# Attention with mixed heads and a two-layer MLP on one core: the step planner counts TensorE's instructions in blocks of 256 and gets new ranks

## The chip, the cores and the metric

The kernel runs on one core of a Trainium2 chip. The metric is device time in microseconds (us), measured outside the profiler; lower is better. Profiles are single executions, so their times are compared with their own span.

## What is computed

```python
def _attn_ref(q, k, v, w_pre, w_post):            # q, k, v: (4, 12, 448, 64) float32
    scale = 1.0 / np.sqrt(q.shape[-1])
    scores = scale * np.matmul(q, k.transpose(0, 1, 3, 2))
    scores = np.einsum('bhij,hg->bgij', scores, w_pre)     # heads mixed, 12 x 12
    scores = scores - np.max(scores, axis=-1, keepdims=True)
    attn = np.exp(scores)
    attn = attn / (np.sum(attn, axis=-1, keepdims=True) + 1e-09)
    attn = np.einsum('bhij,hg->bgij', attn, w_post)        # heads mixed again
    return np.matmul(attn, v)

def _moe_ref(x, U, V, w_ch1, w_ch2):              # x: (4, 448, 768), weights float64
    h = x.transpose(0, 2, 1) @ U @ V              # U 448 x 32, V 32 x 448
    u = x + h.transpose(0, 2, 1)
    return u + np.maximum(u @ w_ch1, 0.0) @ w_ch2 # 768 -> 3072 -> 768
```

The attention output of a batch, heads side by side, is the x of the second function.

## The kernel before

**Two stages.** The first is the attention with its two head mixings; the second is the MLP, with each weight split into a high and a low part and three matmuls for every product (`up`, `dn`). The first stage works in chunks of 10 query rows: 180 chunks over 4 batches, gathered into 17 units of 6 to 12 chunks; two chunks make one `premix`/`postmix` pair, k = 0 to 89. The second runs over 24 slices f of the hidden dimension and the 4 batches b.

**The steps of the first stage, in the order of the data** (line numbers as in the profile):
- `q`, `k`, `v` loads on SP's DMA queue (L378, L371, L498). The k tile of a batch comes in parts, for batches 1 to 3 in six of one head pair each.
- `qk` (TensorE, L394): scores of a unit's rows for one head pair (two pairs in the first two units), into a PSUM bank. `qk_out` (ACT or DVE, helper lines L302/L304) copies the bank into an `s` tile; there are 3 of these.
- `relay` (SP queue, for the first two units half of them on ACT's, L405): two DMAs for each head pair, which carry the s tile to a `t` tile in the layout that the mixing wants. There are two t tiles, which alternate by unit: the relays of unit u can start only when the last `premix` of unit u-2 is done.
- `premix` (TensorE, L432) mixes the heads into a bank; `max` (DVE, L437), two `exp` (ACT, L442), `eps` (POOL, L446), `recip` (DVE, L449), `scale` (POOL, L453) follow; `postmix` (TensorE, L467, 56 small matmuls, each with a weight load) mixes again into another bank; `post_out` (ACT or DVE, L302/L304) copies that into an `a` tile.
- `av` (TensorE, L509 and L517) multiplies with v, twice per unit; `av_out`, `av_add` bring it into the accumulator. When a batch is complete, `tp`, `t1`, `hp` (L707, L724, L738) apply U and V.

All of TensorE's steps share 4 PSUM bank pairs (`bank_58` to `bank_61` in the rows of the order).

**What sets the order.** Nothing is reordered when the kernel runs: each engine and each DMA queue takes its instructions in the order in which they were written. The class `Plan` writes it while the kernel is built. It plays the steps through with a price for each (a table in the code, in ns) and, whenever an engine is free, takes the ready step of lowest rank whose buffers and bank are free. The ranks come from the table `RANK`, in units of chunks. For the change these matter: `qk_lead` and `qk_step` (how many chunks before the unit's first chunk its qk steps are ranked), `kr` and `qr` (how much earlier the loads of k and q are ranked, and at which `premix` they are let go), `av_off` and `av_step` (how long after a unit's last chunk its av steps come), `post`, `ex`, `qo`, and for the first two units `k0`, `kstep`, `k1`. The second stage from f = 2 on follows lists of its own for PE, ACT, DVE and POOL (`plan.lines`), which the change does not touch.

The price of a step on TensorE before was a number alone, with one addition for an engine that had stood idle:

```python
                    if e == "PE" and now - free[e] > 600:
                        cost += min(cost, 850)
```

Of the kernel before, what the change touches and what calls it, by code (L numbers as in the profile page):

```python
# [18 lines left out]
B, H, S, D = 4, 12, 448, 64  # L19
# [11 lines left out]
AV = 3  # L31
# [14 lines left out]
class Unit:  # L46
# [12 lines left out]
RANK = dict(  # L59
    m0=16.083, mb=7.238, mf=2.802, e0=-45.773, estep=6.06, er=6.491, ne=8, qk_lead=5.047, qk_step=0.857, av_off=4.137,  # L60
    av_step=0.796, post=4.408, kr=4.245, vr=7.776, qr=5.202, mx=0.98, ex=1.029, ep=3.308, po=2.298, qo=0.448, 
    uv0=4.57, uvs=0.155, uv1=2.315, u0=-2.242, us=7.039, w0=2.447, w1=22.727, up=-0.694, raw=8, even=2, ga=-0.14, k0=-14.744, kstep=-0.114, k1=8.823,
)
# [28 lines left out]
class Plan:  # L92
# [5 lines left out]
    LATENCY, PE_LATENCY = 128, 196  # L98
    DMA_START, DMA_DONE = 650, 910

    def __init__(self, rings, banked, banks, weight):
# [16 lines left out]
    def take(self, s):  # L118
        ring = self.bank_free if s[0] in self.banked else self.rings[s[0]]
        self.where[s] = ring.pop(0)  # L120

    def order(self):
        steps, users = self.steps, dict(self.users)
# [16 lines left out]
        for k, n in wait.items():  # L140
            if n == 0:
                push(k, 0)

        place = {k: (n, i) for n, line in enumerate(self.lines) for i, k in enumerate(line)}
# [26 lines left out]
        while events:  # L171
# [28 lines left out]
            while moved:  # L200
                moved = False
                for e in free:
# [20 lines left out]
                    if e == "PE" and now - free[e] > 600:  # L223
                        cost += min(cost, 850)
                    if e in self.port[k]:
                        cost += max(0, shared - now)
                        shared = now + cost
# [18 lines left out]
def build(tc, q2, kt, vj, wpre_in, wpost_in, u_in, v_in, ident, w1j, w2, out, show=None):  # L246
# [230 lines left out]
    for k in range(NC // 2):  # L477
        r = 2 * k
        us = sorted({chunks[2 * k][0], chunks[2 * k + 1][0]})
        pre, post, st, e, wr = ("pre", k), ("post", k), ("st", k), ("e", k), ("wr", k)  # L480
        ts = [("t", u) for u in us]
        plan.add(("premix", k), [("PE", 770)], partial(premix, k=k), r, ["wpre", ("zero", 0), ("zero", 1)] + [("relay", u, h) for u in us for h in range(H)], [pre] + ts)
        plan.add(("max", k), [("DVE", 1000)], partial(neg_max, k=k), r + RANK["mx"], [("premix", k)], [pre, st], port=())
        for i in range(2):
            plan.add(("exp", k, i), [("ACT", 622)], partial(exp, k=k, i=i), r + RANK["ex"], [("max", k)], [pre, st, e])
        plan.add(("eps", k), [("POOL", 120)], partial(add_eps, k=k), r + RANK["ep"], [("exp", k, i) for i in range(2)], [st], port=())
        plan.add(("recip", k), [("DVE", 80)], partial(recip, k=k), r + RANK["ep"], [("eps", k)], [st], port=())
        plan.add(("scale", k), [("POOL", 330)], partial(scale_w, k=k), r + RANK["ep"], ["wpost", ("recip", k)], [st, wr], port=BOTH)
        plan.add(("postmix", k), [("PE", 815)], partial(postmix, k=k), r + RANK["post"], [("scale", k)], [e, wr, post])
        for js in ([(0, 1)] if len(us) == 1 else [(0,), (1,)]):  # L490
# [42 lines left out]
    for u, un in enumerate(units):  # L533
# [4 lines left out]
        for p in range(0, H // 2, AV):  # L538
            r = rank_av(u, p)
            z = ("av", (u, p))  # L540
            plan.add(("av", u, p), [("PE", 300 + AV * 610)], partial(av, u=u, p=p), r, [("v", un.b, p + c) for c in range(AV)] + [("post_out", c) for c in range(first[u], first[u + 1]) if ("post_out", c) in plan.steps],
                     [(f"vr{p // AV}", un.b), (f"a{tn(u)}", u), z])
            plan.add(("av_out", u, p), OUT(AV * un.rows), partial(av_out, u=u, p=p), r + 0.65 * AV, [("av", u, p)], [z], port=())
            plan.add(("av_add", u, p), [("DVE", 75 + 1.042 * AV * un.rows // 2)], partial(av_add, u=u, p=p), r + 0.65 * AV, [("av_out", u, p)], [z], port=())
# [400 lines left out]
```

## Time and profile before

| | us |
|---|---|
| time, median of 3 runs | 1080.75 |
| lowest and highest of them | 1076.23, 1084.03 |
| the profiled execution: its own time | 1082.24 |
| its span, first to last instruction | 1080.4 |
| TensorE busy in the span | 1038.6 (96%) |
| DVE, ACT, POOL busy | 679.1, 402.4, 274.2 |
| TensorE's matmuls, weight loads, semaphore rows (counts) | 12240, 12240, 272 |

The page of the profile gives busy time by engine and in 40 slices; other views give waits (who stood idle, and what ended the idle time), a timeline of instructions, the chain of work that ended last, and the busy time in chosen stretches with the clock that TensorE was granted (PEclk, as a share of 2.4 GHz) and the share of the 16 DMA engines. The ends of matmuls are modelled: a matmul is shown as busy until about 0.2 us after the next one could start, so a wait shown as 0.7 us is a gap of about 0.9 us from start to start. "issue" as the releaser of a wait means that no semaphore event ended it.

### The profile page before, as it was taken

Reading aid. Unit: us, or ns where it says so; the run is one execution under the profiler, and the core shown is the slowest. Engines: PE = TensorE matmul, PEld = TensorE weight load, DVE = VectorE, ACT = ScalarE, POOL = GpSimd, SP = SyncE. Lnnn points to the kernel's source line nnn. Section 1 sums busy time; section 2 is a strip of 40 time slices with the busy share of each in tenths; the row PEclk is TensorE's granted clock in tenths of the full one; section 3 lists DMA queues with packets and bytes.
Section 4 is the critical chain, followed back from the end, with each engine's and each line's share of the span. In section 5 each row is a group of like instructions: output and inputs, shape, how many; then the busy total and the mean of one; then the engine's idle time right before and its main releaser. Section 6 shows DMA issues by size and latency. Waiting matters only on the chain.

```text
span 1080.4 us, 28693 instructions
## 1 busy us (share of the span) xinstructions
PE 1038.6 (96%) x12240; PEld 880.4 (81%) x12240; DVE 679.1 (63%) x1091; ACT 402.4 (37%) x844; POOL 274.2 (25%) x395
## 2 busy tenths in 40 slices
PE   4798999999989999999999999999999999999998
PEld 1465666765656788999999999999999999999998
DVE  2274575576567979666666666666666666666635
ACT  1785777667757832122122112221222122212200
POOL 3131111111213813232223223332232233322300
PEclk8999999999999999999999999999999999999999
DMA  6674546545666212121121112211221122212105
GB/s 182 203 202 136 175 143 187 179 140 173 178 192 180 69 52 89 47 71 55 49 59 59 48 56 59 59 59 44 59 59 48 55 59 59 59 44 60 45 1 204
DMA packets 59511, 105.25 MB, mean 97 GB/s; under 512 B 11816, under 2 KB 43768, under 8 KB 59384
## 3 DMA queue, kind: packets, MB, share of 16 engines
q1 hardware_dynamic: 58544, 102.14, 31.9%
q8 instruction: 96, 1.57, 0.6%
q10 hardware_dynamic: 840, 1.29, 0.4%
q14 instruction: 31, 0.25, 0.1%
HBM read 57.62 MB, written 7.08 MB: 60 GB/s over the span
## 4 chain that ended last, share of the span: by engine, by line
PE 88%; DMA 5%; ACT 2%; DVE 2%; issue 1%; SPq 1%; POOL 0%; ACTq 0%; DVEq 0%
PE bank L780 32%; PE bank L800 32%; PE bank L467 6%; PE bank L509 6%; PE bank L394 5%; PE bank L432 4%; DMA t<-s 3%; PE bank L517 1%; ACT e L442 1%; DMA k<-in_kt 1%; PE bank L724 1%; SPq L405 1%; PE bank L707 1%; DMA kr<-in_v 1%; ACT a L302 1%
## 5 line engine op out<-in xcount | busy, mean ns | idle before, releaser
L803 DVE TENSOR_TENSOR acc<-acc,bank 128x896 f32<-128x896 f32 (+1 forms) x153 | 163.7, 1071 | 161.3 <-PE bank L800 160.7
L785 ACT ACTIVATE hh<-bank 128x448 fp32r<-128x448 f32 x96 | 52.3, 545 | 469.0 <-PE bank L780 300.6
L800 PE MATMUL bank<-hh,w1h 128*128 128x448 f32 x576 | 209.1, 363 | 0.0
L780 PE MATMUL bank<-uh,w0h 128*128 128x448 f32 x576 | 209.1, 363 | 0.0
L780 PE MATMUL bank<-ul,w0h 128*128 128x448 f32 x576 | 208.8, 362 | 0.0
L800 PE MATMUL bank<-hl,w1h 128*128 128x448 f32 x576 | 208.7, 362 | 0.0
L780 PE MATMUL bank<-uh,w0l 128*128 128x448 f32 x576 | 207.8, 361 | 0.8 <-POOL w0l L309 0.8
L800 PE MATMUL bank<-hh,w1l 128*128 128x448 f32 x576 | 207.5, 360 | 0.0
L640 POOL TENSOR_TENSOR a<-a,x 128x384 f32<-128x384 f32 (+2 forms) x98 | 98.5, 1005 | 404.7 <-DVE x L636 402.5
L467 PEld LDWEIGHTS bank<-wr,e 60*64 60x64 f32 x5040 | 91.8, 135 | 49.8 <-issue 32.0
L437 DVE TENSOR_REDUCE mx<-bank 128x2 f32<-128x896 f32 x90 | 97.3, 1087 | 36.1 <-PE bank L432 31.1
L442 ACT ACTIVATE e<-bank,mx 128x448 f32<-128x448 f32 x180 | 113.3, 641 | 12.7 <-DVE mx L437 9.3
L800 PEld LDWEIGHTS bank<-hl,w1h 128*128 128x128 f32 x576 | 108.1, 188 | 8.4
L780 PEld LDWEIGHTS bank<-ul,w0h 128*128 128x128 f32 x576 | 108.2, 188 | 8.3
L780 PEld LDWEIGHTS bank<-uh,w0l 128*128 128x128 f32 x576 | 107.7, 187 | 8.6 <-POOL w0l L309 1.0
L800 PEld LDWEIGHTS bank<-hh,w1l 128*128 128x128 f32 x576 | 107.7, 187 | 7.8 <-issue 0.4
L800 PEld LDWEIGHTS bank<-hh,w1h 128*128 128x128 f32 x576 | 108.2, 188 | 5.7
L780 PEld LDWEIGHTS bank<-uh,w0h 128*128 128x128 f32 x576 | 108.1, 188 | 5.7
L467 PE MATMUL bank<-wr,e 60*64 60x60 f32 x5040 | 95.7, 220 | 10.5 <-issue 8.0
L394 PE MATMUL bank<-k,q 64*64 64x448 f32 (+3 forms) x768 | 94.6, 560 | 11.6 <-DMA k<-in_kt 8.2
L789 DVE SCALAR_TENSOR_TENSOR hl<-bank,hh 128x448 fp32r<-128x448 f32 x96 | 60.0, 625 | 66.6 <-ACT hh L785 66.6
L432 PE MATMUL bank<-t,wpre 64*64 64x448 f32 x720 | 87.6, 550 | 13.7 <-DMA t<-s 7.0
(62 smaller groups left out, 1121.6 us busy)
## 6 DMA issues: line engine op xcount, KB each, us to landing
t<-s SPq DMA_DIRECT2D x108, 210.0 KB
kr<-in_w1j SPq DMA_DIRECT2D x48, 384.0 KB
kr<-in_w SPq DMA_DIRECT2D x48, 384.0 KB
v<-in_vj SPq DMA_DIRECT2D x24, 256.0 KB
t<-s SPq DMA_DIRECT2D x24, 192.5 KB
k<-in_kt SPq DMA_DIRECT2D x19, 224.0 KB
t<-s SPq DMA_DIRECT2D x24, 175.0 KB
out<-acc SPq DMA_DIRECT2D x9, 448.0 KB
```

The costliest lines, as they stand in the source:

```text
L394: eng.matmul(o[64 * j:64 * j + at.stop - at.start, i, :S], lhsT=q[d, pp, at], rhs=k[d, pp, :], start=True, stop=True)
L432: eng.matmul(o[64 * j:64 * j + 64, i, :S], lhsT=wpre[64 * i:min(64 * i + 64, QW)], rhs=tt[tn(u)][64 * i:min(64 * i + 64, QW), n, :], start ...
L437: eng.tensor_reduce(out=mx, in_=T["pre", k][:, :, :S], axis=AX.X, op=ALU.max, negate=True)
L442: eng.activation(out=e[:, i], in_=T["pre", k][:, i, :S], func=ACTF.Exp, bias=T["mx", k][:, i:i + 1], accum_out=sm[:, i:i + 1])
L467: eng.matmul(d, lhsT=e[64 * j:64 * j + HALF, i, x * KB:x * KB + KB], rhs=wr[64 * j:64 * j + HALF, i].rearrange("p (g m) -> p g m", m=MH), ...
L509: eng.matmul(main[i * D:(i + 1) * D, c, :n], lhsT=v[:, c, i, x, :], rhs=a[:, x * H + 2 * (p + c) + i, :n], start=(c == 0 and x == 0), stop ...
L640: eng.tensor_tensor(out=f32(a), in0=f32(a), in1=f32(x), op=ALU.add)
L780: eng.matmul(ps, lhsT=w[:, c * 128:(c + 1) * 128], rhs=u[:, c, :], start=(i == 0), stop=(i == 3 * KC - 1))
L785: eng.activation(out=hh, in_=T["up", f, b], func=ACTF.Relu)
L789: eng.scalar_tensor_tensor(out=hl, in0=T.pop(("up", f, b)), scalar=0.0, in1=f32(T["hh", f, b]), op0=ALU.max, op1=ALU.subtract)
L800: eng.matmul(ps[:, j, :S], lhsT=w[:, (c + j) * 128:(c + j + 1) * 128], rhs=h, start=(i == 0), stop=(i == len(todo) - 1))
L803: eng.tensor_tensor(out=two(b, c, n), in0=two(b, c, n), in1=T.pop(("dn", f, b, c))[:, :n, :S], op=ALU.add)
```

## The change

Three things are changed in the planner, and none in what a step does. The planner now counts TensorE's instructions and, 258 instructions after the place 190 of each block of 256 (at the count 448 from that block's start), holds TensorE until 4000 ns have passed since that place (`fetched`). Some prices are new (`premix`, `eps`, `postmix`, and `av`, now by the unit's size). And the table of ranks is new. The diff, its tables cut:

```diff
 RANK = dict(
-    m0=16.083, mb=7.238, mf=2.802, e0=-45.773, estep=6.06, er=6.491, ne=8, qk_lead=5.047, qk_step=0.857, av_off=4.137,
-    av_step=0.796, post=4.408, kr=4.245, vr=7.776, qr=5.202, mx=0.98, ex=1.029, ep=3.308, po=2.298, qo=0.448, 
+    m0=15.987, mb=7.238, mf=0.142, e0=-47.025, estep=5.816, er=6.491, ne=8, qk_lead=3.034, qk_step=0.905, av_off=7.445,
+    av_step=1.166, post=4.081, kr=3.495, vr=7.776, qr=5.96, mx=0.98, ex=1.386, ep=3.308, po=2.298, qo=-0.27, 
...
     DMA_START, DMA_DONE = 650, 910
+    BLOCK, ASKED, NEEDED, FETCH = 256, 190, 448, 4000
...
+    def instructions(self, k):
+        fixed = dict(qk=16, premix=16, postmix=112, av=120, tp=16, t1=16, hp=4)
+        return fixed[k[0]] if k[0] in fixed else round(self.steps[k][0][0][1] / 100)
...
+        count, asked = 0, {}
+
+        def fetched(n, t, cost):
+            nonlocal count
+            late = 0
+            for i in range(1, n + 1):
+                j, x = divmod(count + i, self.BLOCK)
+                if x == self.ASKED:
+                    asked[j] = t + late + cost * i / n
+                j, x = divmod(count + i - self.NEEDED + self.ASKED, self.BLOCK)
+                if x == self.ASKED and j in asked:
+                    late = max(late, asked.pop(j) + self.FETCH - t - cost * i / n)
+            count += n
+            return late
...
                     if e == "PE" and now - free[e] > 600:
                         cost += min(cost, 850)
+                    if e == "PE":
+                        cost += fetched(self.instructions(k), now, cost)
...
-        plan.add(("premix", k), [("PE", 770)], ...
+        plan.add(("premix", k), [("PE", 790)], ...
...
-        plan.add(("eps", k), [("POOL", 120)], ...
+        plan.add(("eps", k), [("POOL", 190)], ...
...
-        plan.add(("postmix", k), [("PE", 815)], ...
+        plan.add(("postmix", k), [("PE", 900)], ...
...
-            plan.add(("av", u, p), [("PE", 300 + AV * 610)], ...
+            plan.add(("av", u, p), [("PE", 735 + 138 * un.n)], ...
```

The number of instructions is the same but for semaphore rows (272 of TensorE's before, 267 now); what moves is their order. In the rows below, line numbers are those of each kernel (the change shifts them by 22), `x24` counts the matmuls of the program, of which the trace shows two records for each in these steps, and names such as `bank_59`, `s_165`, `t_141` are buffers.

TensorE in the first microseconds, before: the premix of pair 3, postmix 1, premix 4, postmix 2, premix 5 and the first av.

```order
L432 MATMUL bank_60<-t_141,wpre 64x448 x4
L467 MATMUL bank_59<-wr_287,e_265 64x12x5 x24
L467 MATMUL bank_59<-wr_287,e_265 64x60 x4
L432 MATMUL bank_59<-t_141,wpre 64x448 x4
L467 MATMUL bank_60<-wr_334,e_280 64x12x5 x24
L467 MATMUL bank_60<-wr_334,e_280 64x60 x4
L432 MATMUL bank_60<-t_141,wpre 64x448 x4
L509 MATMUL bank_59<-a_325,v_236 64x60 x18
```

The same pairs now, premix 3 to premix 5:

```order
L454 MATMUL bank_58<-t_141,wpre 64x448 x4
L489 MATMUL bank_60<-wr_304,e_255 64x12x5 x24
L489 MATMUL bank_60<-wr_304,e_255 64x60 x4
L416 MATMUL bank_59<-k_151,q_206 64x448 x2
L416 MATMUL bank_59<-k_151,q_206 60x448 x2
L454 MATMUL bank_61<-t_141,wpre 64x448 x4
L416 MATMUL bank_60<-k_151,q_206 64x448 x2
L416 MATMUL bank_60<-k_151,q_206 60x448 x2
L489 MATMUL bank_59<-wr_324,e_297 64x12x5 x24
L489 MATMUL bank_59<-wr_324,e_297 64x60 x4
L454 MATMUL bank_58<-t_141,wpre 64x448 x4
```

Before, premix 4 takes the bank of the postmix just ahead of it, and premix 5 again; now a qk step lies between a postmix and the next step in its bank. The first two av steps, one of which followed premix 5, come after postmix 5 now.

TensorE where batch 1 begins, before: three qk steps of unit 5 (k_962 is the k tile of batch 1), premix 19 to 21, two postmix steps.

```order
L394 MATMUL bank_59<-k_962,q_200 64x448 x2
L394 MATMUL bank_59<-k_962,q_200 50x448 x2
L432 MATMUL bank_61<-t_142,wpre 64x448 x4
L467 MATMUL bank_60<-wr_287,e_265 64x12x5 x24
L467 MATMUL bank_60<-wr_287,e_265 64x60 x4
L394 MATMUL bank_58<-k_962,q_200 64x448 x2
L394 MATMUL bank_58<-k_962,q_200 50x448 x2
L432 MATMUL bank_60<-t_142,wpre 64x448 x4
L467 MATMUL bank_58<-wr_334,e_280 64x12x5 x24
L467 MATMUL bank_58<-wr_334,e_280 64x60 x4
L432 MATMUL bank_61<-t_142,wpre 64x448 x4
L432 MATMUL bank_59<-t_142,wpre 64x448 x4
```

The same place now, from premix 19 on:

```order
L454 MATMUL bank_59<-t_142,wpre 64x448 x4
L489 MATMUL bank_60<-wr_324,e_297 64x12x5 x24
L489 MATMUL bank_60<-wr_324,e_297 64x60 x4
L416 MATMUL bank_61<-k_1006,q_206 64x448 x2
L416 MATMUL bank_61<-k_1006,q_206 50x448 x2
L454 MATMUL bank_58<-t_142,wpre 64x448 x4
L489 MATMUL bank_60<-wr_253,e_237 64x12x5 x24
L489 MATMUL bank_60<-wr_253,e_237 64x60 x4
L454 MATMUL bank_61<-t_142,wpre 64x448 x4
L416 MATMUL bank_59<-k_1006,q_206 64x448 x2
L416 MATMUL bank_59<-k_1006,q_206 50x448 x2
L489 MATMUL bank_60<-wr_304,e_255 64x12x5 x24
```

Before, premix 20 and 21 stand side by side ahead of an av step (L509, the next row); now a postmix stands between them, premix 21 is followed by the unit's last qk, and the av step comes two steps later. Relative to the premix steps, the qk steps come later.

SP's queue at the same place, before: the last relays of unit 4 (t_142), those of unit 5 (t_141) and the loads of k for batch 1.

```order
L371 DMA k_962<-in_kt 128x448
L405 DMA t_142<-s_185 10x9x448 x2
L371 DMA k_962<-in_kt 128x448
L405 DMA t_141<-s_165 10x11x448 x2
L405 DMA t_141<-s_173 10x11x448 x2
L405 DMA t_141<-s_185 10x11x448 x2
L371 DMA k_962<-in_kt 128x448
L378 DMA q_148<-in_q 128x372
```

And now:

```order
L393 DMA k_1006<-in_kt 128x448 x2
L427 DMA t_142<-s_165 10x9x448 x2
L427 DMA t_141<-s_181 10x11x448 x2
L427 DMA t_141<-s_179 10x11x448 x2
L393 DMA k_1006<-in_kt 128x448
L400 DMA q_148<-in_q 128x372
L427 DMA t_141<-s_165 10x11x448 x2
L393 DMA k_1006<-in_kt 128x448
L427 DMA t_141<-s_181 10x11x448 x2
```

The fifth load of k was ahead of unit 5's relays and is now behind two pairs of them; the sixth stays behind three pairs, with the load of q between.

## Rows read from the trace of the kernel before

**Rows 1.** Busy time by stretch: us, busy of each engine, PEclk, DMA share, GB/s

```profile
7.00:54.00 47.00, 33.87 (x682) 17.86 (x684) 15.77 (x23) 23.05 (x45) 6.29 (x13) 0.93 0.63 192
54.00:373.00 319.00, 302.43 (x7840) 205.82 (x7836) 210.56 (x345) 230.31 (x508) 72.56 (x192) 0.99 0.56 165
411.00:1056.00 645.00, 645.00 (x3227) 604.69 (x3225) 410.03 (x670) 132.68 (x264) 177.57 (x174) 1.00 0.19 54
```

**Rows 2.** TensorE's waits over the span, four of 17 lines: total us, times, longest

```profile
PE bank L394 <- DMA k<-in_kt: 8.2, 2, 7.0
PE bank L467 <- issue: 8.0, 13, 2.2
...
PE bank L432 <- ACT s L302: 3.6, 2, 3.0
...
PE bank L467 <- POOL wr L453: 0.4, 1, 0.4
```

**Rows 3.** Timeline of TensorE, four steps: start us, us, ..., count [idle before]

```profile
59.87 0.33 PE L467 MATMUL bank<-wr,e 60*64 60x60 f32 x4 [0.73 <-issue]
60.13 1.26 PE L509 MATMUL bank<-a,v 128*64 128x60 f32 x36
61.33 0.55 PE L517 MATMUL bank<-a,v 64*64 64x30 f32 x24
61.70 0.96 PE L432 MATMUL bank<-t,wpre 64*64 64x448 f32 x8
62.48 0.98 PE L467 MATMUL bank<-wr,e 60*64 60x60 f32 x55
63.76 0.21 PE L467 MATMUL bank<-wr,e 60*64 60x60 f32 x1 [0.29 <-issue]
```

**Rows 4.** DMA queues, the one that brings instructions: packets, MB, share

```profile
q8 instruction: 96, 1.57, 0.6%
```

**Rows 5.** Timeline of TensorE, a stretch without waits

```profile
231.75 0.93 PE L394 MATMUL bank<-k,q 64*64 64x448 f32 x8
232.50 0.99 PE L467 MATMUL bank<-wr,e 60*64 60x60 f32 x56
233.31 0.94 PE L432 MATMUL bank<-t,wpre 64*64 64x448 f32 x8
```

**Rows 6.** Timeline of TensorE, postmix 2 and premix 5

```profile
35.90 1.04 PE L467 MATMUL bank<-wr,e 60*64 60x60 f32 x56 [0.31 <-issue]
37.91 0.98 PE L432 MATMUL bank<-t,wpre 64*64 64x448 f32 x8 [0.97 <-ACT a L302]
```

**Rows 7.** The page's costliest groups, two of them: busy us, mean ns, idle before

```profile
L437 DVE TENSOR_REDUCE mx<-bank 128x2 f32<-128x896 f32 x90 | 97.3, 1087 | 36.1 <-PE bank L432 31.1
L442 ACT ACTIVATE e<-bank,mx 128x448 f32<-128x448 f32 x180 | 113.3, 641 | 12.7 <-DVE mx L437 9.3
```

**Rows 8.** Premix 21: TensorE's timeline, the chain of work, and the stretch behind it

```profile
97.96 0.98 PE L432 MATMUL bank<-t,wpre 64*64 64x448 f32 x8 [2.95 <-ACT s L302]
98.87 3.73 PE L509 MATMUL bank<-a,v 128*64 128x120 f32 x36
89.38 7.52 DMA t<-s
98.00:102.00 4.00, 4.00 (x40) 3.29 (x42) 1.33 (x3) 2.38 (x8) 1.16 (x4) 0.62 0.55 170
```

**Rows 9.** Last qk step of unit 9: the chain of work, and TensorE's timeline

```profile
181.88 6.49 DMA k<-in_kt
188.50 0.98 PE L394 MATMUL bank<-k,q 64*64 64x448 f32 x8 [1.16 <-DMA k<-in_kt]
```

**Rows 10.** Unit 16's last qk, an av, unit 16's first premix, timeline of TensorE

```profile
345.74 0.94 PE L394 MATMUL bank<-k,q 64*64 64x448 f32 x8
...
347.42 2.07 PE L509 MATMUL bank<-a,v 128*64 128x120 f32 x36
...
349.82 0.94 PE L432 MATMUL bank<-t,wpre 64*64 64x448 f32 x8
```

More of the change, by code (lines that the diff above doesn't have):

```diff
@@ L59 @@
 RANK = dict(
-    m0=16.083, mb=7.238, mf=2.802, e0=-45.773, estep=6.06, er=6.491, ne=8, qk_lead=5.047, qk_step=0.857, av_off=4.137,
-    av_step=0.796, post=4.408, kr=4.245, vr=7.776, qr=5.202, mx=0.98, ex=1.029, ep=3.308, po=2.298, qo=0.448,
-    uv0=4.57, uvs=0.155, uv1=2.315, u0=-2.242, us=7.039, w0=2.447, w1=22.727, up=-0.694, raw=8, even=2, ga=-0.14, k0=-14.744, kstep=-0.114, k1=8.823,
+    m0=15.987, mb=7.238, mf=0.142, e0=-47.025, estep=5.816, er=6.491, ne=8, qk_lead=3.034, qk_step=0.905, av_off=7.445,
+    av_step=1.166, post=4.081, kr=3.495, vr=7.776, qr=5.96, mx=0.98, ex=1.386, ep=3.308, po=2.298, qo=-0.27,
+    uv0=1.213, uvs=0.155, uv1=2.598, u0=-5.605, us=10.351, w0=-0.219, w1=22.496, up=-0.694, raw=8, even=2, ga=-0.391, k0=-15.092, kstep=0.284, k1=17.484,
 )
@@ L481, in build @@
         ts = [("t", u) for u in us]
-        plan.add(("premix", k), [("PE", 770)], partial(premix, k=k), r, ["wpre", ("zero", 0), ("zero", 1)] + [("relay", u, h) for u in us for h in range(H)], [pre] + ts)
+        plan.add(("premix", k), [("PE", 790)], partial(premix, k=k), r, ["wpre", ("zero", 0), ("zero", 1)] + [("relay", u, h) for u in us for h in range(H)], [pre] + ts)
         plan.add(("max", k), [("DVE", 1000)], partial(neg_max, k=k), r + RANK["mx"], [("premix", k)], [pre, st], port=())
@@ L485, in build @@
             plan.add(("exp", k, i), [("ACT", 622)], partial(exp, k=k, i=i), r + RANK["ex"], [("max", k)], [pre, st, e])
-        plan.add(("eps", k), [("POOL", 120)], partial(add_eps, k=k), r + RANK["ep"], [("exp", k, i) for i in range(2)], [st], port=())
+        plan.add(("eps", k), [("POOL", 190)], partial(add_eps, k=k), r + RANK["ep"], [("exp", k, i) for i in range(2)], [st], port=())
         plan.add(("recip", k), [("DVE", 80)], partial(recip, k=k), r + RANK["ep"], [("eps", k)], [st], port=())
         plan.add(("scale", k), [("POOL", 330)], partial(scale_w, k=k), r + RANK["ep"], ["wpost", ("recip", k)], [st, wr], port=BOTH)
-        plan.add(("postmix", k), [("PE", 815)], partial(postmix, k=k), r + RANK["post"], [("scale", k)], [e, wr, post])
+        plan.add(("postmix", k), [("PE", 900)], partial(postmix, k=k), r + RANK["post"], [("scale", k)], [e, wr, post])
         for js in ([(0, 1)] if len(us) == 1 else [(0,), (1,)]):
@@ L540, in build @@
             z = ("av", (u, p))
-            plan.add(("av", u, p), [("PE", 300 + AV * 610)], partial(av, u=u, p=p), r, [("v", un.b, p + c) for c in range(AV)] + [("post_out", c) for c in range(first[u], first[u + 1]) if ("post_out", c) in plan.steps],
+            plan.add(("av", u, p), [("PE", 735 + 138 * un.n)], partial(av, u=u, p=p), r, [("v", un.b, p + c) for c in range(AV)] + [("post_out", c) for c in range(first[u], first[u + 1]) if ("post_out", c) in plan.steps],
                      [(f"vr{p // AV}", un.b), (f"a{tn(u)}", u), z])
```

## The prediction

> **What bounds the kernel now.** I read the busy time by stretch first [rows 1]. From 411 to 1056 us TensorE is busy in every microsecond, at full clock: the second stage runs on lists that the change doesn't touch, so nothing is to be had there. From 7 to 54 us TensorE is idle for 47.0 - 33.9 = 13.1 us, from 54 to 373 us for 319.0 - 302.4 = 16.6 us. The reader is to see that the first stage alone can move, and that its visible idle time is some 30 us; no other engine is above 230.3 of 319.0 us there, so none of them bounds it by its sum. Then the waits of TensorE [rows 2]: the largest are loads at the very start, 8.0 us of "issue" inside postmix steps, 3.6 us for a copy of `s`, and a tail of small ones for a bank that a copy or an exp still holds (11.9 us in all lines that name ACT's, DVE's or POOL's work ahead of a bank or a weight, of 17 lines from the first to the last shown, without the two for `t` and `w0l`).
>
> **"issue" is the fetch of TensorE's instructions.** The queue that brings them moved 1.57 MB in 96 packets, 16 KB each [rows 4], for 24,480 matmuls and weight loads and 272 semaphore rows: 256 to a packet. And two waits in a row stand that far apart: 4 + 36 + 24 + 8 + 55 = 127 matmuls, each with its weight load, lie between the wait at 59.87 and that at 63.76 us, 254 instructions and two semaphores in 3.89 us [rows 3]. So a stretch that issues 256 instructions in less than about 4 us stalls; a postmix issues 112 in 0.81 us, a qk 16 in 0.75 us [rows 5].
>
> The Trainium skill ("Runtime: NRT & Kernel Launch", section on instruction fetch mechanics) says that the next block is fetched while the current one runs, and that crossing a block costs little and is mostly hidden. The trace does not agree: 13 waits, 8.0 us [rows 2]. By the page the fetch term below would be 0 and the sum 1.6 us lower.
>
> **Term 1, the fetch: +1.6 us.** The change means to price exactly this. But its count leaves the semaphore rows out: 272 of them shift the blocks by up to 272 places, a whole block, by the end of the first stage, so the planner moves steps to mend stalls that stand elsewhere. I counted both orders with the semaphores: for each block the work between its place 190 and the place 258 instructions on, each step by its start-to-start time (qk and premix 0.75, postmix 0.81 [rows 5], an av of 12 chunks 2.4 [rows 10], smaller ones in proportion), and what this lacks to 4.0 us. Before: 18 blocks lack 9.7 us together; after: 22 lack 11.1. (Without the semaphores, as the planner counts: 8.8 before, 7.1 after.) For scale: the 13 waits show 8.0 us, and each hides 0.2 us more, since a matmul is shown busy for 0.93 us and the next step starts after 0.75 [rows 5]; 10.6 us against 9.7 counted. After: 10.6 x 11.1 / 9.7 = 12.2, so +1.6. Bounds: -10.6 (all of it goes, if the planner's blocks are right) and +4 (a stall like those shown costs 0.3 to 2.2 us [rows 2, 3]; two more of them).
>
> **Term 2, banks held by copies and exps: -8.7 us.** A step that takes a bank needs the former one's data out of it. Postmix 2 starts at 35.90; with 0.81 us it would be over at 36.71, and premix 5, which takes the same bank at once, starts at 37.91 [rows 6]: 1.2 us. For qk I take 1.25 (the same path), for premix 2.9: the max 1.09, two exps 0.64 each [rows 7], and some 0.5 for the read of the sums and the hand-overs. In the order of before, 19 steps of the first stage and its end come too early for their bank, 11.5 us in sum; in the new order 6, 2.8 us. The two pieces at the start show it: premix 4 and 5 each directly behind the postmix in their bank, 1.2 us each, and now a qk step between. The sum agrees with what the waits show without premix 21's: 11.9 - 3.0 [rows 2], and 0.2 hidden in each of 18 waits, 12.5 us. So 11.5 - 2.8 = 8.7. Bounds: 0 (see the second rival) and -12.5.
>
> **Term 3, premix 21: -3.0 us.** It waited 2.95 us for a copy [rows 8]: its bank held the scores of unit 5, whose copy wanted an `s` tile that relays still read, and one of those took 7.52 us to land [rows 8], because unit 5's relays all start together when their `t` tile comes free. The av behind it ran at a clock of 0.62 and took 3.73 us [rows 8], where one of its size takes 2.07 [rows 10]: 1.66 us more. With `qk_lead` at 3.0 fewer qk steps run ahead of the free tile, and the step that takes the bank of the unit's fourth qk comes 7.8 us after it is free, not 6.2. If the relay again takes 7.5 us this covers 1.6 of the 2.95, if 6 us all of it. I take 3.0 of the 4.6. Bounds 0 and -4.6.
>
> **Term 4, loads of k: +2.4 us.** `kr` falls from 4.2 to 3.5. The last loads of a batch are let go 4.6 to 6.2 us of TensorE's work ahead of their qk now, and on SP they stand behind relays that wait themselves; what is left is 4.6 to 5.4 us for five of the six. Before, one that took 6.49 us was 1.16 late [rows 9], so 5.3 would have been in time there. At 5.8, between these two, 0.4 to 1.2 us are missing at each; I take 1.2 for each of the three batches, since a stall gives the next load time: 3.6, less the 1.2 that goes. Bounds: -1.2 (loads land in 4 us) and +6.
>
> **What costs nothing.** The first loads of k are turned round (small part first): the first qk needs 672 KB either way. The loads of v have 10 us or more of TensorE's work before their av, where the slowest landing shown is 7.5 [rows 8]. The new prices change the plan alone. The lists from f = 2 on stay, and work at the seam (postmix 86 to up 1) is the same but for steps that change places.
>
> **Sum.** 1.6 - 8.7 - 3.0 + 2.4 = -7.7 us. The profiled execution took 1082.2 us (span 1080.4 and 1.8 around it): 1074.5. It lies 1.5 us above the median, so against the median 1080.75 the forecast is **1073 us**, from 1064 to 1080 by itself.
>
> **Rivals.**
> - *The fetch pricing works.* If the first blocks matter most, where the semaphores have shifted little, or the planner spreads postmix steps widely enough, term 1 is -10.6 and not +1.6: 1073 - 12 = 1061. For it: waits of this kind lie early too, as those of rows 3, where few semaphores have been passed. Against: my count, by which in the first 50 us of work 6 blocks of the new order lack 4 us, and 4 blocks of the old one 3 us.
> - *The waits come back as fetch.* A bank wait ahead of a fetch stall hides part of it: TensorE issues nothing while it waits, and the block lands meanwhile. Taken away, the same stall shows. If three quarters of term 2 are eaten so, +6.5: 1079.5. For it: a block takes 5.2 us on average (15,676 matmuls and weight loads in 319 us [rows 1]), not far above 4. Against: 18 blocks lack time, of the 66 in the first stage, so most bank waits stand in others.
> - *Relays come too late* (the other side). The last qk of a unit now ends 4.8 to 6.3 us of work ahead of the unit's first premix in 10 units, before 6.3 to 9.4. Its path: the copy, 1.2 us; the first relay's issue, 0.8; the landing of the second. In the old order, unit 16, this took at most 349.82 - (345.74 + 0.75) = 3.3 us [rows 10], so a landing of 1.3 us, and then nothing waits. But with the 6.49 or 7.52 us of rows 8 and 9 the need is 8.4 to 9.5 us, and with 5.8 us 7.8: 1.5 to 3 us missing in 11 units, some 20 us. Then 1073 + 20 = 1093. It decides from about 4.6 us of landing on, where it takes back the 7.7 us. For it: DMA share 0.56 over the whole stage [rows 1]. Against: rows 10, and that loads and relays that late stand where DMA had a pile of work.
>
> **Chances.** My forecast 0.46, fetch pricing works 0.18, waits come back 0.23, relays late 0.13. Range: it reaches up to 1088, which leaves out most of the relays' case, and down to 1058, which leaves out the lower part of the fetch's; 0.15 lie outside. What a measurement can tell from no change is about 1%, 10.8 us: below 1069.9 is faster, above 1091.6 slower. Faster: the fetch case and a third of mine, 0.18 + 0.16 = 0.34. Slower: the relays' case, 0.13, most of which lies that high. The rest, 0.53, is no difference.
>
> **What the profile after would show.** Term 1: "issue" ahead of postmix between 8 and 10 us; under 3 us would prove the first rival. Term 2: the lines that name ACT, DVE and POOL ahead of banks at some 3 to 5 us where they were 11.9; if they fall and "issue" rises by as much, the second rival is right. Term 3: no wait of 3 us ahead of a premix between 90 and 100 us, and no stretch there at 0.62. Term 4: waits for `k<-in_kt` of 2 to 5 us beside the 7.0 at the start, at the fifth and sixth qk of units 5, 9 and 13. The third rival would show as premix steps waiting for `t<-s` at the first premix of many units. The stretch where TensorE is busy without a gap should begin 7 to 8 us earlier, and be as long as before; if it is not, something at the seam is wrong with my reading.

## The result, and the profile after

| | before | after |
|---|---|---|
| time, median of 9 runs each (us) | 1080.75 | 1086.56 |
| lowest and highest | 1076.23, 1084.03 | 1081.88, 1089.78 |
| ratio, 95% interval | | 1.0057 [1.0033, 1.0082] |
| the profiled execution: its own time, span | 1082.24, 1080.4 | 1083.71, 1081.9 |
| TensorE's granted clock, mean of the span in the profile | 0.994 | 0.994 |
| the same, mean over the timed runs | 0.995 (29 runs, of a later comparison) | 0.992 (9 runs) |

The changed kernel is slower, by 0.3 to 0.8%. That is less than the 1% named in the prediction, inside its range, and on the other side of its forecast of 1073 us. The profiled execution of after lies 2.9 us below the median of its runs, the one of before 1.5 us above its own, so the two traces differ by 1.5 us where the medians differ by 5.8. A second profile of each was taken (under "Both kernels once more" below): after, 1.0 us below the median of its runs, before, 5.1 us above its own. So the rows show where the two orders wait, but not the whole of the 5.8 us. What is said of a place rests on both profiles.

Busy time by stretch, after (columns as in [rows 1]):

```profile
7.00:54.00 47.00, 34.52 (x652) 16.31 (x652) 17.02 (x23) 20.86 (x43) 6.28 (x13) 0.93 0.67 191
54.00:373.00 319.00, 299.22 (x7851) 203.97 (x7848) 205.39 (x339) 231.87 (x513) 65.20 (x185) 0.99 0.56 165
411.00:1056.00 645.00, 645.00 (x3225) 604.69 (x3226) 407.06 (x663) 132.13 (x263) 175.80 (x173) 1.00 0.18 53
```

The second stage is as it was: 645.00 of 645 us busy. From its 201st matmul of `up` to its last of `dn` it takes 622.2 us in all four profiles, and this stretch begins 1.5 us later than before (1.3 us in the second pair), where the prediction had 7 to 8 us earlier. From 54 to 373 us TensorE is idle for 19.8 us, before for 16.6 [rows 1]. The loss is in the first stage, where the gain was to be.

TensorE's waits over the span, after, the lines that matter (engine, line, waited for: us in total, times, longest):

```profile
PE bank L416 <- DMA k<-in_kt: 9.2, 5, 5.1
PE bank L454 <- DMA t<-s: 7.0, 2, 6.1
PE bank L489 <- issue: 6.4, 6, 2.5
PE bank L454 <- ACT s L324: 2.0, 2, 1.0
...
PE bank L531 <- DMA v<-in_vj: 1.3, 1, 1.3
PE bank L454 <- DMA v<-in_vj: 1.3, 1, 1.3
PE bank L454 <- ACT uh L324: 1.2, 1, 1.2
PE bank L454 <- ACT acc L324: 1.2, 1, 1.2
```

Against [rows 2]: the lines for ACT, DVE and POOL together are 9.9 us, before 13.6 (11.9 without `t` and `w0l`, as the prediction took them). The loads have become more: k waits beyond the first one of the start are 4.1 us where they were 1.2, and v waits 2.6 us where there were none. "issue" is 8.0 us over four lines, before 8.8.

**The wait that the view misnames.** Four of these copies' waits (two "ACT s", "ACT uh", "ACT acc", 4.4 us) stand ahead of the *first* premix of a unit. Such a premix needs the unit's t tile, which the last relay fills. TensorE's timeline after, the first premix of units 7, 11 and 16 with the steps ahead, and SP's queue at unit 7's last relays (start, us, ...):

```profile
156.66 0.93 PE L416 MATMUL bank<-k,q 64*64 64x448 f32 x8
158.63 0.98 PE L454 MATMUL bank<-t,wpre 64*64 64x448 f32 x8 [1.03 <-ACT s L324]
...
244.64 0.92 PE L416 MATMUL bank<-k,q 64*64 64x448 f32 x8
246.42 0.98 PE L454 MATMUL bank<-t,wpre 64*64 64x448 f32 x8 [0.85 <-DMA t<-s]
...
356.39 0.58 PE L539 MATMUL bank<-a,v 64*64 64x60 f32 x24
358.21 0.98 PE L454 MATMUL bank<-t,wpre 64*64 64x448 f32 x8 [1.24 <-ACT uh L324]
```

```profile
153.15 1.56 SPq L427 DMA_DIRECT2D t<-s  x2
```

The same wait carries three names here: a copy of `s` that ended just then, the relay, a copy of the MLP's input. What tells it from a real wait for a bank is the transfer. The second of the two issues, unit 7's last relay, began at 153.96; its last packet ended at 157.59 and the premix started at 158.63, that is 4.67 us from issue to use. In units 9, 11, 15 and 16 the premix starts 0.73 to 1.13 us behind the last relay packet too, 4.3 to 5.5 us behind the issue. The same premix 34 before, without a wait:

```profile
155.51 0.93 PE L394 MATMUL bank<-k,q 64*64 64x448 f32 x8
156.26 0.93 PE L432 MATMUL bank<-t,wpre 64*64 64x448 f32 x8
```

The semaphore events in the traces settle it. They show when the semaphore that a relay raises was last updated. In four profiles with this order of steps (the two of after, and the two with small matmuls ahead, below), wherever one of the six first premix steps of units 7, 9, 11, 14, 15 and 16 (premix 34, 45, 57, 73, 79, 85) waits, it starts at a fixed time behind the last update for its unit's last relay: 0.35, 0.24, 0.14, 0.30, 0.31 and 0.46 us, each the same within 0.01 us. The waits themselves are 0.46 to 3.66 us long, and the view names them after copies (`s`, `acc`, `uh`), relays, loads of q, a transfer of `a`, or "issue". In the two profiles of before the six start 0.36 to 4.86 us behind that update, and none waits for it.

The longest is premix 73's in the second profile of after, 3.66 us under the name "issue". The last relay of its unit took 9.5 us from its issue to the last update (8.4 in the first profile); before, it took 8.5 and 6.7 us, and premix 73 came 13.4 and 10.3 us behind the issue.

Counted from start to start, less the step's own length, these six premix steps lose 7.2 us together after and 8.7 in its second profile; before 1.5 and 1.8, nearly all of it at premix 85, ahead of which a block of instructions came late. This is the prediction's third rival, at a third of its price.

**Where batch 1 begins**, after (the place of [rows 8]): postmix 17, the fifth qk of unit 5, then the stretches on either side (columns as in [rows 1], the clock third from the end):

```profile
95.54 0.56 PE L489 MATMUL bank<-wr,e 60*64 60x60 f32 x19 [2.51 <-issue]
97.72 1.76 PE L416 MATMUL bank<-k,q 64*64 64x448 f32 x8 [1.62 <-DMA k<-in_kt]
99.23 1.74 PE L454 MATMUL bank<-t,wpre 64*64 64x448 f32 x8
```

```profile
98.00:104.00 6.00, 6.00 (x88) 3.06 (x85) 2.45 (x4) 1.71 (x6) 0.58 (x2) 0.55 0.28 83
92.00:98.00 6.00, 1.87 (x68) 1.52 (x64) 1.93 (x3) 2.98 (x8) 0.58 (x2) 0.88 0.69 206
```

The 3 us wait ahead of premix 21 is gone. In its place a block of instructions came late, then a load of k, and after these two waits TensorE ran at a clock of 0.55 for 6 us: the steps of 0.75 us start 1.5 us apart.

### The profile page after: what moved, and what is told of

Read it like the earlier page. It is cut to its first block, busy times and chain, and to the rows that moved or that the text cites. A ratio compares the mean times of both kernels' runs of the same rounds, so it can differ in the third digit from the quotient of the medians.

```text
span 1081.9 us, 28683 instructions
## 1 busy us (share of the span) xinstructions
PE 1040.0 (96%) x12240; PEld 879.5 (81%) x12240; DVE 675.3 (62%) x1085; ACT 404.8 (37%) x853; POOL 271.7 (25%) x392
## 4 chain that ended last, share of the span: by engine, by line
PE 65%; DVE 2%; ACT 1%; issue 0%; DVEq 0%
PE bank L822 31%; PE bank L802 31%; PE bank L531 1%; PE bank L489 1%; PE bank L454 0%; DVE acc L825 0%; DVE acc L766 0%; ACT e L464 0%; PE bank L539 0%; DVE xl L331 0%; PE bank L729 0%; DVE x L658 0%; DVE a L653 0%; ACT s L324 0%; PE bank L416 0%
## 5 line engine op out<-in xcount | busy, mean ns | idle before, releaser
L662 POOL TENSOR_TENSOR a<-a,x 128x384 f32<-128x384 f32 (+2 forms) x95 | 95.5, 1005 | 397.4 <-DVE x L658 392.3
L464 ACT ACTIVATE e<-bank,mx 128x448 f32<-128x448 f32 x180 | 113.8, 642 | 21.4 <-DMA t<-s 11.6
L416 PE MATMUL bank<-k,q 64*64 64x448 f32 (+3 forms) x768 | 98.0, 567 | 10.5 <-DMA k<-in_kt 9.2
L454 PE MATMUL bank<-t,wpre 64*64 64x448 f32 (+1 forms) x720 | 90.5, 560 | 14.9 <-DMA t<-s 7.0
```

Of the source, the lines that this page charges most:

```text
L416: eng.matmul(o[64 * j:64 * j + at.stop - at.start, i, :S], lhsT=q[d, pp, at], rhs=k[d, pp, :], start=True, stop=True)
L454: eng.matmul(o[64 * j:64 * j + 64, i, :S], lhsT=wpre[64 * i:min(64 * i + 64, QW)], rhs=tt[tn(u)][64 * i:min(64 * i + 64, QW), n, :], start ...
L464: eng.activation(out=e[:, i], in_=T["pre", k][:, i, :S], func=ACTF.Exp, bias=T["mx", k][:, i:i + 1], accum_out=sm[:, i:i + 1])
L662: eng.tensor_tensor(out=f32(a), in0=f32(a), in1=f32(x), op=ALU.add)
```

## The experiments

Ratios are to the kernel before, run on the same chip in the same comparison, with 95% intervals; medians of 6 to 12 runs against 23 to 35.

**Both kernels once more.**

> The changed kernel once more, on the same chip as the three others, for a second profile: the first profiled execution of it was 2.9 us below the median of its runs. The ratio to before should come out within 1.0033 to 1.0082 again. If its loss lies in fixed places, the same waits stand in this profile: the one for issue and the one for k at 95 to 98 us, the half clock until 104, the later first premix. If the loss lies in transfers that vary from run to run, a slower execution shows larger or other waits for loads, relays and issue, and the same waits for banks.

1.0054 [1.0031, 1.0077], 1084.31 us. The loss is the order's own. In this profile the first premix steps wait as before (34: 1.3, 57: 1.0, 79: 0.6, 85: 1.7 us, premix 73 even 3.8), k is late again, and the fetch at 95 us was in time. TensorE's timeline there, and at two other places, then the stretches behind those two (columns as in [rows 1]):

```profile
92.43 1.36 PE L489 MATMUL bank<-wr,e 60*64 60x60 f32 x56
94.42 0.97 PE L416 MATMUL bank<-k,q 64*64 64x448 f32 x8 [0.63 <-DMA k<-in_kt]
95.19 0.95 PE L454 MATMUL bank<-t,wpre 64*64 64x448 f32 x8
...
268.01 0.97 PE L416 MATMUL bank<-k,q 64*64 64x448 f32 x8 [3.36 <-DMA k<-in_kt]
...
303.27 1.92 PE L454 MATMUL bank<-t,wpre 64*64 64x448 f32 x8 [3.66 <-issue]
```

```profile
268.00:273.00 5.00, 4.99 (x84) 3.04 (x88) 2.25 (x3) 1.36 (x4) 0.58 (x2) 0.66 0.44 137
302.00:307.00 5.00, 3.73 (x67) 3.02 (x68) 1.09 (x1) 0.27 (x1) 0.00 (x0) 0.66 0.64 183
```

So what the order fixes is where something is tight; which of these places costs 0 or 4 us differs from one execution to the next. Behind these two waits, 3.36 us for a load of k and 3.66 us for a relay, the clock fell too: 0.66 over 5 us. Of the waits named "issue" in this profile,

```profile
PE bank L454 <- issue: 4.1, 2, 3.7
PE bank L489 <- issue: 3.3, 5, 1.4
```

the first line is premix 73 and premix 79, both waiting for relays. With 1.0 us in two smaller lines, 4.3 of 8.4 us are left for the fetch.

> The kernel before, unchanged, as one more entry beside the three others: what this method shows for no change at all, and a second profile of it. The ratio should be 1.000 with an interval of 0.002 to either side. If it comes out at 1.002 or above, the 0.3% that several edits cost is no more than the method's own scatter. In the profile, waits for the same buffers at the same steps as in the first one are the order's own; those that come and go are the transfers'.

0.9998 [0.9971, 1.0025], 1076.92 us: the method shows no change as none. Its profile has, at the place of [rows 8], no 2.95 us ahead of premix 21 but this:

```profile
98.98 1.47 PE L467 MATMUL bank<-wr,e 60*64 60x60 f32 x56 [1.99 <-DVE s L304]
100.16 3.03 PE L432 MATMUL bank<-t,wpre 64*64 64x448 f32 x16
```

Two premix steps that take 3.03 us where 1.7 is usual: the same place, another step, 3.3 us lost in these two rows.

**Six swaps: are the waits for the relays?** After, with the first premix of six units behind the step that followed it on TensorE:

```diff
     order = plan.order()
+    for n in (34, 45, 57, 73, 79, 85):
+        at = [i for i in range(len(order)) if order[i][1] == "PE"]
+        i = next(j for j, x in enumerate(at) if order[x][0] == ("premix", n))
+        order.insert(at[i + 1], order.pop(at[i]))
```

> The changed kernel with one edit of TensorE's list: the first premix of six units (premix 34, 45, 57, 73, 79, 85), each of which waited 1.0 to 1.4 us in the profile after, changes places with the step behind it. If these waits are for the last relay (in the profile after these premix steps start 0.7 to 1.1 us after the last relay packet, in the one before 1.2 us or more), the step behind fills about 0.75 us of each: 4 to 4.5 us, ratio to before 1.0015, and nothing waits ahead of these six by more than 0.5 us. If the waits are for the bank or the copy that the profile names (ACT s, ACT acc, ACT uh), the step put ahead waits in its place or the next one does, and the ratio stays at 1.0055.

1.0022 [1.0003, 1.0041], 1079.41 us: 0.33% of the 0.55% came back, from one edit of six places (0.1 to 0.6% when the runs of the three comparisons are resampled). Its timeline at unit 7 and unit 16:

```profile
154.67 0.99 PE L489 MATMUL bank<-wr,e 60*64 60x60 f32 x56
156.09 0.98 PE L454 MATMUL bank<-t,wpre 64*64 64x448 f32 x8 [0.43 <-DMA t<-s]
...
349.21 1.04 PE L489 MATMUL bank<-wr,e 60*64 60x60 f32 x56 [0.39 <-POOL wr L475]
350.15 1.73 PE L454 MATMUL bank<-t,wpre 64*64 64x448 f32 x16
```

The postmix runs in the time that was a wait, what is left of premix 34's now carries the relay's name, and unit 16's is gone; the six lose 2.1 us, not 7.2. One wait is longer than expected, premix 79's with 0.75 us. The copies named there were not the cause.

**One rank half way back**: after, with `qk_lead=4.047`.

> The changed kernel with one rank half way back, qk_lead 4.047 in place of 3.034; the planner lays all steps again. In the list that comes out, the last qk of a unit ends 7.0 us of work or more ahead of the unit's first premix in all units from 2 on but one (5.5); short of the 6.65 us that the path took: 1.2 us in sum, 8.4 in the changed kernel, 1.1 before. Banks by the count of term 2: 6.8 us short (2.8 changed, 11.7 before); fetch by count 11.6 (11.1 changed, 9.7 before). If the late relays are what ate the gain of the banks, this kernel has 19.6 us short in sum against 22.3 in the changed one and 22.5 before: ratio 1.000 to 1.003, and no first premix waits for over 0.5 us but one or two. If relays don't matter, the banks' 4 us more are lost: 1.007 to 1.010.

1.0054 [1.0024, 1.0084], 1084.26 us (1074 to 1089, the widest of all), between the two values expected. In the profile, of an execution 7.0 us below that median, the first premix steps of the six lose 0.8 us, as foreseen; lines for ACT, DVE and POOL are 9.9 us, all of them real now, where 9.9 - 4.4 = 5.5 were after. In this profile what the relays give back the banks take: the two look like one trade, set by how far ahead the qk steps run. Whether the sum is a gain this run can't tell.

**The place of the blocks.** After and before with small matmuls ahead of everything, while TensorE waits for the first loads (52 or 28 of them, 208 or 112 instructions); all else stands, and what they write is overwritten by the first qk:

```diff
+    one = sb["wc"].tile([1, 8], F32, "one")
...
+        nc.vector.memset(one, 0.0)
+        for _ in range(52):
+            nc.tensor.matmul(BANKS[0][0:1, 0, 0:1], lhsT=one[:, 0:1], rhs=one[:, 0:1], start=True, stop=True)
```

> The changed kernel with 52 matmuls of one element at the head of TensorE's list, while it waits for the first loads; nothing else moves. They are 208 instructions with their weight loads, and push every block boundary of the fetch to another place: 208 is 48 short of a block, about what the semaphore rows had added by the middle of the first stage, so the planner's own count nearly holds again. By my count of work between asking and needing a block the lack falls from 11.1 to 6.9 us. If the fetch term was mis-sized because the planner left the semaphore rows out, this gains 3 to 4 us on the changed kernel: ratio to before 1.002, issue waits down by 3 us or more. If the time of a fetch is set by other traffic and not by 4 us, placing by count is worth nothing: ratio 1.0055 as before the shift.

1.0036 [1.0013, 1.0059], 1080.80 us.

> The changed kernel with 28 such matmuls, 112 instructions, by which my count of the lack rises from 11.1 to 11.6 us. It is the control of the run with 208: if a gain there comes from the place of the blocks, none is seen here, ratio 1.0055 to 1.006. If it comes from something else that the small matmuls do (an earlier clock, a later start), both show it alike.

1.0075 [1.0045, 1.0105], 1084.19 us. Waits for "issue", first with 208, then with 112 instructions ahead:

```profile
PE bank L490 <- issue: 4.1, 3, 3.7
```

```profile
PE bank L490 <- issue: 6.2, 5, 2.4
PE bank L532 <- issue: 2.9, 3, 1.3
PE bank L417 <- issue: 1.2, 1, 1.2
PE bank L540 <- issue: 0.6, 2, 0.4
```

4.1 against 10.9 us, with one order of the steps, which without the shift has 8.0 and 4.3 us. The two times lie 0.4% apart, about what the two counts (6.9 and 11.6 us) differ by, but their intervals overlap, and that the place of the blocks makes the difference is not shown: the two profiled executions took the same, 1083.1 and 1083.4 us, and in them the six first premix steps lost 10.2 us with 208 and 5.6 us with 112. The Trainium skill ("Runtime: NRT & Kernel Launch", section on instruction fetch mechanics) has this cost mostly hidden. That holds here for most of the blocks (96 without the shift [rows 4]); in 3 places of the first profile and 11 of the second TensorE waits.

> The kernel before with 28 such matmuls, 112 instructions: my count of the lack falls from 9.7 to 7.5 us. By a fixed time of 4 us for a block this gains 2 us: ratio to before 0.998, which would beat both kernels. If other traffic sets the time of a block, the ratio is 1.000 within 0.002, with the stalls in other places.

0.9984 [0.9959, 1.0008], 1074.29 us.

> The kernel before with 112 more instructions ahead, a second time on another chip or hour: the first gave 0.9984 [0.9959, 1.0008]. If the place of the blocks is worth the 2.2 us of my count, the ratio is 0.998 again and the two together exclude 1. If it was scatter, it is 1.000.

0.9963 [0.9944, 0.9982], 1072.06 us: faster than both kernels.

> The kernel before with 52 small matmuls ahead, 208 instructions: by my count of blocks the lack is 9.2 us, where it is 9.7 without and 7.5 with 112. It is the control of the gain that 112 showed (0.9984 and 0.9963). If the place of the blocks makes that gain, the ratio to before is 0.9995 within 0.002. If the small matmuls themselves do (by an earlier clock, or anything else at the start), it is 0.997 again.

0.9970 [0.9946, 0.9994], 1073.27 us. The control gained too, where my count gave it nothing. Its waits for "issue":

```profile
PE bank L468 <- issue: 2.1, 3, 1.6
PE bank L510 <- issue: 0.6, 1, 0.6
```

2.7 us, where the kernel before has 8.8 and 9.8 and the two profiles with 112 have 5.8 and 4.8. The mean clock of the timed runs is 0.996 with 208, against 0.994 for before in the same comparison. So on the kernel before time and fetch waits fall together under both shifts, but the count with a fixed 4.0 us doesn't say by how much. That the small matmuls help in some other way is not excluded there; with 112 on the changed kernel they did not.

> The changed kernel with both repairs, 208 more instructions ahead and the six swaps. If the fetch (worth 0.2% there, 1.0036 against 1.0055) and the late relays (4 us) are separate losses that add up, the ratio to before is 1.000. If one hides behind the other, the ratio is 1.002 to 1.0036, and issue waits come back by 2 us or more over the 4.1 and 0.9 us of the run with the shift alone.

1.0031 [1.0010, 1.0052], 1079.70 us: in time the two don't add. In the profile both losses are smaller: "issue" reads 5.8 us, but 2.0 of it is premix 73's wait for its relay, so the fetch waits are 3.8, not above the 4.1 of the shift alone; and the six premix steps lose 3.2 us where they lost 10.2. The time is that of the expectation's second case, but its sign, fetch waits that come back, is not seen; why the time fell no further stays open.

**Without the planner's delay for the fetch.** After, the two lines that call `fetched` left out.

> The changed kernel without the delay that the planner now adds for the fetch; new ranks and new prices of the steps stay. If counting the fetch is what places the steps of the changed kernel well, taking it away costs: the ratio to before is 1.008 to 1.011, as for the new ranks under the old planner, and issue waits rise by 3 us or more. If the delay, counted without the semaphore rows, only mislays steps, the ratio falls to 1.001 to 1.004. If it matters little, the ratio stays at 1.0057 within 0.002.

1.0073 [1.0050, 1.0097], 1085.89 us, "issue" 14.7 us, of which

```profile
PE bank L452 <- issue: 4.8, 2, 4.1
```

is premix 73 and premix 79 again, which start 0.30 and 0.31 us behind the last update for their relays. That leaves 9.9 us of fetch waits where after has 8.0 and 4.3: the delay does some of what it is for. The time lies 0.2% above after's, with overlapping intervals.

**Each half alone.** New planner and prices with the old table of ranks:

> The old table of ranks with the new planner (fetch count and prices). Theory A: the old ranks keep their early loads, so about the time of the kernel before, 1077 to 1084. Theory B (the count of instructions misleads the planner): slower than before by as much as the whole change or more, 1085 or over.

1.0103 [1.0065, 1.0140], 1090.05 us: "issue" falls to 5.6 us, but ACT, DVE and POOL are named for 18.7.

New ranks with the old planner and prices:

> The new table of ranks with the old planner and old prices. Theory A (late loads come from the ranks): slower than before, 1084 to 1092, with waits for k and for relays. Theory B (the planner's count does the harm): about the time before or better, under 1082.

1.0083 [1.0054, 1.0111], 1089.13 us: "issue" 12.2 (1.1 of it premix 79's relay), ACT, DVE and POOL 15.6. Either half alone has a higher median than both together, though the intervals overlap. The same ranks under another planner give another order.

**Loads of k earlier.** Ten places up SP's list, on after, on before, and on after with the swaps:

```diff
+    for n, step in enumerate(order):
+        if step[0][0] == "k" and step[0][1]:
+            before = [i for i in range(n) if order[i][1] == "SP"]
+            order.insert(before[-10], order.pop(n))
```

> The changed kernel with one thing moved: on SP's queue the loads of k for batches 1 to 3 stand 10 places earlier, ahead of the relays that they followed; the order of the computing engines is the same. Theory A (the bank gain was lost to loads and relays that the new ranks start late): the two waits for k (3.3 us together) go, and the half-clock stretch behind the one at 97 us (98 to 104 us at 0.55) shrinks, so 4 to 6 us less than the changed kernel. Theory B (the loss is in TensorE's order itself, banks and fetch): within 1.5 us of the changed kernel.

1.0037 [1.0009, 1.0065], 1082.82 us; k waits 5.9 us instead of 9.2, "issue" 12.6 (0.9 of it premix 57's relay) instead of 8.0.

> The kernel before, with each load of k for batches 1 to 3 moved 10 places up SP's list; all other lists as they were. If loads of k that come late are a loss of their own (in the kernel before one was 1.16 us late), this gains that and no more: ratio to before 0.998 to 1.000. If earlier loads only push the relays and the instruction fetch back by what they win, the ratio is 1.000 to 1.003, the waits for k are gone and the waits named issue or t<-s are 1 to 3 us higher. If the same edit brings 0.2% here too, as it did on the changed kernel, the lateness of k is not what tells the two kernels apart.

1.0033 [1.0012, 1.0055], 1080.93 us. On the kernel before the same edit *costs* 0.3%: k waits fall by 1.5 us, "issue" rises from 8.8 to 10.9.

> The changed kernel with the six swaps, which gave 1.0022, and with the loads of k for batches 1 to 3 ten places earlier, which alone gave 1.0037 where the changed kernel has 1.0055. If late k loads are a third separate loss, the two add up: 1.0004. If earlier loads win at their own place and lose it again to relays and fetch, the ratio is 1.002 to 1.003.

1.0010 [0.9987, 1.0033], 1078.56 us: no longer told from before. The intervals with and without the earlier loads overlap, so the second edit's share is not shown by time.

**The first loads.** After with the old `k0`, `kstep`, `k1`, alone and with k early:

> The changed kernel with the three old ranks of the first two units (k0, kstep, k1). Theory A with the start as one of its places: the first premix, 1.8 us later than before in the changed kernel, comes at 20.3 us again, and the time falls by about 2 us. If the start is no part of it: within 1 us of the changed kernel, but for what the planner reorders behind.

1.0034 [1.0008, 1.0060], 1081.77 us.

> The changed kernel with both repairs that each seemed to give back 0.2%: loads of k for batches 1 to 3 ten places earlier, and the three old ranks for the first loads of k. If the two losses are separate and add up, the ratio to before is 1.001 (1.0057 - 0.0020 - 0.0023). If each repair only shuffles many small waits, the two together are no better than one: 1.003 to 1.005.

1.0031 [1.0008, 1.0053], 1081.24 us: the two don't add. The three ranks move steps all over the first stage (the first premix of unit 2 waits 0.1 us instead of 1.5, that of unit 14 4.3 instead of 1.3), so this says little on the start itself.

## Why the prediction was wrong

**The step that failed is in the third rival: "Against: rows 10".** I read 3.3 us at most from unit 16's last qk to its first premix, so 1.3 us for a relay to land, gave the rival 0.13, and put nothing for it in the sum. But the premix at 349.82 in [rows 10] is premix 83, of unit 15. Unit 16 begins with premix 85, in the same timeline of before:

```profile
354.14 1.74 PE L432 MATMUL bank<-t,wpre 64*64 64x448 f32 x16
```

That is 7.65 us behind the end of the last qk, not 3.3. Taken right, the row says nothing against the rival: it leaves room for a path that in the profile after takes 2.0 to 2.5 us from the last qk's end to the last relay's issue and 4.3 to 5.5 us from there, 6.3 to 8.0 in sum. The prediction had put the point where the rival decides at 4.6 us of landing, and three of the five units measured have 4.65 to 4.69. With 6.65 us needed, and the work that lies between the two steps in each unit, the new order is 8.4 us short, the old one 1.1: +7.3, where the profiles show +5.7 and +6.8. That the sums are so near is partly luck: 1.8 of the 8.4 us stand in unit 3, which lost almost nothing, and unit 14, not short by this count, lost 1.4 and 3.8 us, since its relays took 8.4 and 9.5 us. The swaps show the relays in time: 3.6 us of 5.9.

**Term 2, -8.7: nearly right, and eaten.** Without the misnamed waits and the second stage's, the lines of ACT, DVE and POOL are 4.5 us where they were 11.9; in the second profiles 4.4 against 10.4. Without the waits at premix 21's place (2.95 and 1.99 us), which are term 3's, that is 4.4 and 4.0 us less, and with the 0.2 us hidden in each of the ten and seven waits that are gone 6.4 and 5.4. I treated it as a gain by itself, when the same rank that frees the banks (`qk_lead` from 5.0 to 3.0, qk steps later against the premix steps) is what makes the relays late.

**Term 3, -3.0: right in one execution of two.** From premix 18 to premix 22 the losses are 7.0 and 4.6 us before, 7.5 and 1.7 after. So the mean fell by 1.2 us, but the place is tight in both orders, and in the first profile of after the fetch and k took what the copy had taken. "No stretch there at 0.62" failed with 0.55. A single wait in one trace was read as a property of the order.

**Term 4, +2.4: right.** Beyond the start, k waits are 3.3 us in two after and some 4.0 in its second profile, 1.2 and 0 before.

**Term 1, +1.6: sign wrong, within its bounds.** Without the waits for relays, "issue" is 8.0 and 4.3 us after, 8.8 and 9.8 before, so about -3, with a spread as large. The count takes 4.0 us for each block; from the asking place to the resumed step I measure 2.9 to 9.6 us at the stalls of the first stage after. The transfer itself takes 0.9 to 1.6, and it begins 0.6 to 6.9 us after the asking place. What it costs that the count leaves the semaphore rows out is not shown: 208 more instructions, which set the blocks nearly where the planner believes them, gave 1.0036, and that interval holds the 1.0055 without them.

**"Costs nothing": the loads of v.** They waited 2.6 and 1.7 us at the first av steps, where I had 10 us of work. Yet up to premix 6 both orders lose the same (26.3 and 28.1 us before, 27.2 and 26.9 after), so the start as a whole is no part of the loss.

**What stays open.** Terms 1 to 4, the relays and the loads of v, as measured, give -3 - 6 - 1 + 3 + 6 + 2 = 1, and the profiles differ by 1.4 us. Some waits stand in two of these (the stretch from premix 18 to 22 holds waits for the fetch and for k), so that is agreement to 2 or 3 us and no better. The medians differ by 5.8. In the timed runs the mean clock is 0.992 after and 0.995 before, and 0.003 of 1081 us is 3 us; over the 35 runs of the kernel before in one comparison, 0.001 of clock goes with 1.0 us. The profiles don't show this difference (0.994 and 0.992 in both orders), so which waits lower the clock in the executions without a trace is not known. Some 2 us more have no place at all.

## What to carry to other kernels

A wait that a change removes should be followed to the next buffer on the same data's way: here qk steps that come later leave the banks sooner and fill the t tile too late, and the two prices are one term. Where a view names a copy that ended just then, or "issue", look for a transfer that landed in the same microsecond; a wait that ends at the same distance from one transfer in every profile is a wait for it. And look up by the step's number which unit a row belongs to. And a wait seen in one execution of a kernel whose transfers crowd is a tight place, not a fixed cost: take two profiles before pricing it.

## What was not expected of the hardware

- Pushing all block boundaries by 112 or 208 instructions, with no step moved, made the kernel before 0.2 to 0.4% faster (0.9963, 0.9970, 0.9984; the last interval reaches 1.0008). On after, 1.0036 and 1.0075 are not told from 1.0055.
- Where a premix waits for a relay, it starts 0.7 to 1.1 us after the relay's last packet and 0.14 to 0.46 us after the last semaphore update, the same time for each premix in four profiles. From issue to that update a relay took 3.8 to 5.2 us in five units and 8.4 and 9.5 us in unit 14.
- In the two profiles of after, waits of 3.36 and 3.66 us, and two of 2.51 and 1.62 us close together, were followed by stretches at a granted clock of 0.55 to 0.66, so for the most part at the lower level, 1.2 GHz: steps of 0.75 us took 1.5. The length of a wait alone does not say it: one of 2.11 us with `qk_lead=4.047` was followed by 0.66 over 5 us, one of 2.91 us with k early, ahead of premix 79, by 1.00. No such stretch was left between 54 and 373 us in the fastest profile, that of before with 112 instructions ahead:

```profile
54.00:373.00 319.00, 307.64 (x8054) 210.53 (x8047) 217.00 (x353) 232.27 (x511) 77.71 (x195) 1.00 0.56 167
```
